# Two score tiles in a row at the start of batch 1, and one pair of transposes moved by a group of tiles

## The chip, the cores and the metric

The kernel runs on one core of one Trainium2 chip. The metric is the device time of a run in microseconds (us). The core has five engines that run side by side, each through its own instructions in order: PE (TensorE, matmuls; its weight loads are shown as PEld), ACT (ScalarE), DVE (VectorE), POOL (GpSimd) and SP (SyncE, which here only issues DMAs).

## What is computed

Attention over 8 batches of 12 heads, 448 rows, 64 columns, with normalised queries and keys, and then two matmuls with a tanh GELU between them:

```python
q_n = q / sqrt(mean(q*q, axis=-1) + 1e-6) * g_q      # k_n likewise with g_k
scores = q_n @ k_n.T / 8                             # per batch and head: 448 x 448
attn = exp(scores - max) / sum                       # softmax over the keys
x = attn @ v                                         # then laid out as 3584 x 768
out = gelu_tanh(x @ w_in) @ w_out                    # 768 -> 2048 -> 768
```

## The kernel before

**Stages.** Batch 0's attention and the first matmul of its rows are written out in a string `FRONT` (L891). From batch 1 on, each batch has two strings of tokens in `STEPS` (L643), split at a bar. The part ahead of the bar is the batch's attention; among its tokens stand pieces of the *second* matmul of the batch before. The part behind the bar is the batch's *first* matmul, and the loop from L957 runs them in turn. The order of these tokens is the program order of every engine: the schedule is manual, so nothing is reordered later, and an engine whose next instruction waits holds up all that stand behind it.

**Tokens** (`run`, L657). `s` makes the next score tile: four matmuls of 64x64 (L335), and one exponential on ACT over 128 x 896 (L326). A batch has 21 tiles, three *chunks* of four heads with seven tiles each, so tile 7 is the first of chunk 1. Below they are s0 to s20, and e0 to e20 are their exponentials. `A1` pops one step of part A of the second matmul of the batch before (four matmuls of 64x64 on 384 columns, L447); `A9` pops nine. `a` adds an exponential into its chunk's running sum on DVE (L362); for the first tile of a chunk it does nothing. `S`, `x`, `R`, `X` are the sums, the products with v, the reciprocals and the scaled results. Every third `s` closes a group of tiles: ahead of its first tile `side` work is issued, behind its last tile `end` work.

**PSUM.** Score tiles, transposes, the second matmul's parts B and on, and the first matmul's tiles share three places of two banks (L305 to L320), handed out strictly in turn. `place` takes the next one; the tile in it waits until the former tile there has been read. Part A lives in two other banks.

**Part A.** Its 32 steps come in two turns of 16. Between them the kernel puts a no-operation on POOL (`turned`, L455 to L457) that waits for PE's 16th step and that the 17th step waits for.

**Heads and chunks.** Pairs of heads are numbered 0 to 5. Pairs 2 and 3 make chunk 1 of keys and queries. In batch 1 their normalised rows are transposed on PE (`both_transposed`, L908: four matmuls of L259 and three or four of L266 into one place), and DVE copies them out (`place_q` L276, `place_k` L285). Chunk 2 of batch 1 is normalised on DVE (`normed`, L247, four instructions), transposed by two DMAs that SP issues (`transposed`, L294 and L290), and SP then issues the four loads of batch 2's first chunk (`loads(2, 0)`, L121 and L138). Its squares are taken on ACT later in the same attention (`squared`, L207).

**What the end of a group does in batch 1's attention** is in the dictionary `here` (L961): entry (g, 0) runs first at the end of group g, (g, 1) last. In the kernel before, both pairs of transposes are run at the end of group 0, behind s2.

Of the kernel before, what the change touches and what calls it, by code (L numbers as in the profile page):

```python
# [16 lines left out]
def kernel(  # L17
# [11 lines left out]
    nc = tc.nc  # L29
# [81 lines left out]
    def slots(j):  # L111
        return slice(0, NK) if j == 0 else slice(NK, NS)
# [71 lines left out]
    def view(n, t, j=None):  # L184

        if n == "q":
            return t if j is None else t[:, 2 * j:2 * j + 2]
        return t if j is None else t[:, :, slots(j)]
# [22 lines left out]
    def stat(t, b, c, n, j=None):  # L211

        if b == 0:
            ns = NQ if n == "q" else NK + j
            at = 14 * j + (0 if n == "q" else 8)
            return t[:P if n == "q" else 128, c, at:at + 2 * ns].rearrange("p (a t) -> p a t", a=2)
        if n == "q":
            s = t[:P, c, :CH * NQ].rearrange("p (h t) -> p h t", h=CH)
            return s if j is None else s[:, 2 * j:2 * j + 2]
        s = t[:, c, CH * NQ:].rearrange("p (a s) -> p a s", a=2)  # L220
        return s if j is None else s[:, :, slots(j)]
# [18 lines left out]
    def normed(b, c, n, j, eng):  # L240
        if (n, b, c) not in nrms:
            shape = [P, 2, NQ, 2, D] if n == "q" else [128, NS, 2, D]
            nrms[n, b, c] = nrmp.tile(shape, BF16, tag=f"nrm{n}", name=f"nrm{n}")
        t = nrms[n, b, c]
        dst = t[:, j] if n == "q" else t[:, slots(j)]
        r = stat(rinvs[b], b, c, n, j)
        eng.tensor_mul(  # L247
            dst.rearrange("p t a d -> p a t d"), view(n, raws[n, b, c], j),
            r.to_broadcast(list(r.shape) + [D]),
        )  # L250

    def trans(b, hp, n, pool, tag=None):
        c, j = hp // 2, hp % 2
        tp = pool.tile([128, 1024], BF16, tag=tag, name="tp") if tag else pool
        if n == "q":
            if hp == 0:
                qT[b] = qkp.tile([128, HP, S], BF16, tag="qT", name="qT")
            for t in range(NQ):
                nc.tensor.transpose(  # L259
                    tp[:, t * P:(t + 1) * P],  # L260
                    nrms[n, b, c][:, j, t].rearrange("p a d -> p (a d)"), ident[:P, :P],
                )
        else:
            s = slots(j)
            for i in range(s.stop - s.start):
                nc.tensor.transpose(  # L266
                    tp[:, i * 128:(i + 1) * 128],
                    nrms[n, b, c][:, s.start + i].rearrange("p a d -> p (a d)"), ident,
                )
        return tp  # L270
# [34 lines left out]
    def place(name):  # L305
        i = unused.pop(0)
        t = spots[i].tile([128, 2, 512], F32, tag="sc", name=name)
        taken.append((t, i))
        return t
# [304 lines left out]
    def m2_parts(b):  # L614
# [26 lines left out]
    homes = []  # L641

    STEPS = {  # L643
# [264 lines left out]
    def both_transposed(b, hp):  # L908

        home = place("tp")  # L910
        tp = home[:, 0].bitcast(BF16)
        for n, at in (("q", 0), ("k", 512)):
            tps[n, b, hp] = trans(b, hp, n, tp[:, at:at + 512])
        place_q(b, hp, tps["q", b, hp], nc.vector)
        place_k(b, hp, tps["k", b, hp], nc.vector)
        leave(home)
# [40 lines left out]
    for b in range(B):  # L957
        m1, side, early, late, here = [], [], [], [], {}
        if b == 0:

            here = {(0, 0): [lambda: both_transposed(1, 2), lambda: rsqrt(1, slice(2, NCH))],  # L961
                    (0, 1): [lambda: both_transposed(1, 3)] +
                            [lambda j=j, n=n: normed(1, 2, n, j, nc.vector)
                             for j in range(2) for n in "qk"] +
                            [lambda: transposed(1, 2)] +
                            [lambda: loads(2, 0)]}
# [114 lines left out]
```

## Time and profile before

| | |
|---|---|
| median of 3 runs | 402.72 us |
| fastest, slowest run | 401.46 us, 403.55 us |
| the profiled execution's own time | 400.14 us |
| its span, first to last instruction | 398.1 us |
| mean granted TensorE clock | 0.994 |
| PE, ACT, DVE, POOL busy | 388.9, 304.1, 243.7, 137.8 us |

In the timeline each row is a start, a duration, an engine, a line, what is written and read, and a count of instructions merged; a bracket gives the engine's idle time before the row and what ended it. Rows of one engine may overlap by some tenths of a microsecond, because its instructions are pipelined: a matmul of 448 columns has a duration of 0.35 us, and the next group can start 0.19 us after it. So PE's stalls are read from the starts of its rows rather than from its busy share.

### The profile page before, as it was taken

What the parts mean: (1) busy time and instruction counts of PE and PEld (TensorE: products, weight loads), DVE (VectorE), ACT (ScalarE), POOL (GpSimd) and SP (SyncE); (2) the same over time, 40 slices, a digit from 0 to 9 for tenths busy, and PEclk for the clock granted to TensorE, in tenths of its full rate; (3) what the DMA queues carried; (4) which work ended last, traced back from release to release, by engine and by line L of the source; (5) the groups of instructions that cost most, each with busy time, mean ns of one, the idle gap of its engine ahead of it and who ended that gap; (6) DMA issues with size and microseconds to landing.
All of it is one profiled execution on the core that took longest, in us unless ns stands there. A gap on an engine that the chain in (4) does not pass through costs nothing.

```text
span 398.1 us, 16991 instructions
## 1 busy us (share of the span) xinstructions
PE 388.9 (98%) x7572; PEld 285.5 (72%) x7572; DVE 243.7 (61%) x409; ACT 304.1 (76%) x409; POOL 137.8 (35%) x166
## 2 busy tenths in 40 slices
PE   7899999999999999999999999999999999999996
PEld 3444557878887678766788888776788889776664
DVE  5889829994897456864489635882399503690010
ACT  4897889968999779976997559985999258984400
POOL 5789002151321772155501646246420740000000
PEclk9899999999999999999999999999999999999999
DMA  8999999997947892939683398749743291210022
GB/s 181 227 237 204 205 204 213 242 252 133 166 105 151 204 192 33 216 84 214 85 160 104 91 215 104 162 130 200 105 66 90 76 122 28 68 56 3 2 81 79
DMA packets 75800, 54.63 MB, mean 137 GB/s; under 512 B 41680, under 2 KB 72272, under 8 KB 75728
## 3 DMA queue, kind: packets, MB, share of 16 engines
q1 hardware_dynamic: 59968, 41.69, 49.7%
q0 software_dynamic: 15440, 11.80, 20.3%
q8 instruction: 59, 0.97, 1.1%
q14 instruction: 13, 0.11, 0.1%
q10 hardware_dynamic: 320, 0.07, 0.1%
HBM read 45.61 MB, written 11.01 MB: 142 GB/s over the span
## 4 chain that ended last, share of the span: by engine, by line
PE 94%; ACT 2%; DMA 1%; SPq 1%; DVE 1%; issue 0%; ACTq 0%; DVEq 0%; POOLq 0%
PE hh L447 27%; PE om L447 17%; PE o L447 13%; PE mm L447 10%; PE sc L335 7%; PE o L552 5%; PE hh L523 4%; PE so L447 4%; ACT ex L326 1%; PE sc L351 1%; PE ox L386 1%; DMA rawk<-in_k_dram 1%; PE o L386 1%; PE h L523 1%; PE tp L266 1%; PE tp L259 1%
## 5 line engine op out<-in xcount | busy, mean ns | idle before, releaser
L326 ACT ACTIVATE ex<-sc,shift 128x896 bf16<-128x896 f32 x168 | 156.8, 1015 | 3.7 <-PE sc L351 2.1
L447 PE MATMUL hh<-xT,win 64*64 64x448 bf16 x2304 | 129.8, 349 | 0.7 <-issue 0.7
L447 PEld LDWEIGHTS <-g 64*64 64x64 bf16 x3072 | 108.4, 107 | 21.4 <-POOLq L456 1.2
L447 PEld LDWEIGHTS <-win 64*64 64x64 bf16 x2688 | 94.5, 106 | 33.7 <-ACTq L456 10.9
L447 PE MATMUL om<-wout,g 64*64 64x384 bf16 x1664 | 103.5, 322 | 0.0
L447 PE MATMUL mm<-wout,g 64*64 64x384 bf16 x704 | 86.0, 323 | 0.1
L447 PE MATMUL o<-wout,g 64*64 64x384 bf16 x704 | 85.2, 323 | 0.3 <-ACT g L532 0.3
L532 ACT ACTIVATE g<-hh 128x896 bf16<-128x896 f32 x55 | 49.7, 915 | 34.2 <-PE hh L447 31.7
L224 DVE TENSOR_REDUCE ss<-sq 128x14 f32<-128x896 f32 (+4 forms) x45 | 48.0, 1081 | 27.5 <-ACT sq L207 27.4
L362 DVE TENSOR_TENSOR es<-es,ex 128x896 bf16<-128x896 bf16 x92 | 57.0, 620 | 9.9 <-ACT ex L326 4.1
L335 PE MATMUL sc<-qT,kT 64*64 64x448 bf16 x600 | 57.0, 352 | 0.1
L920 POOL COPY mark<-es 1x1 bf16<-1x1 bf16 x27 | 8.9, 329 | 129.9 <-DVE es L362 109.4
L247 POOL TENSOR_TENSOR nrmq<-rawq,rinv 112x512 bf16<-112x512 f32 x35 | 36.4, 1054 | 30.7 <-DMA qT<-nrmq 23.7
L247 POOL TENSOR_TENSOR nrmk<-rawk,rinv 128x512 bf16<-128x512 f32 (+1 forms) x34 | 32.1, 959 | 2.3 <-ACT rinv L233 1.3
L362 DVE TENSOR_TENSOR es<-ex 128x896 bf16<-128x896 bf16 x21 | 12.9, 612 | 30.6 <-ACT ex L326 30.3
L447 PE MATMUL o<-xT,win 64*64 64x448 bf16 x192 | 31.5, 349 | 0.0
L447 PE MATMUL mm<-xT,win 64*64 64x448 bf16 x192 | 31.3, 349 | 0.0
L335 PEld LDWEIGHTS <-kT 64*64 64x64 bf16 x600 | 24.5, 106 | 8.3 <-issue 2.4
L300 DVE TENSOR_SCALAR kT<-kT,gcol 128x896 bf16<-128x896 bf16 x19 | 14.8, 777 | 23.7 <-DMA kT<-nrmk 23.7
L447 PEld LDWEIGHTS <-vt 64*64 64x64 bf16 x588 | 20.5, 107 | 6.2
L447 PE MATMUL o<-ex,vt 64*64 64x448 bf16 x182 | 20.8, 349 | 0.0
L447 PE MATMUL mm<-ex,vt 64*64 64x448 bf16 x182 | 20.5, 349 | 0.0
(112 smaller groups left out, 451.3 us busy)
## 6 DMA issues: line engine op xcount, KB each, us to landing
rawq<-in_q_dram SPq DMA_DIRECT2D x48, 224.0 KB, 5.2
rawk<-in_k_dram SPq DMA_DIRECT2D x42, 224.0 KB, 5.3
vt<-in_v_dram POOLq DMA_DIRECT2D x24, 168.0 KB, 4.3
win<-in_moe_w_in_dram POOLq DMA_DIRECT2D x4, 768.0 KB, 12.0
wout<-in_moe_w_out_dram POOLq DMA_DIRECT2D x4, 768.0 KB, 20.9
out_dram<-osb SPq DMA_DIRECT2D x7, 336.0 KB, 4.4
out_dram<-osb SPq DMA_DIRECT2D x8, 288.0 KB, 2.7
out_dram<-osb SPq DMA_DIRECT2D x8, 240.0 KB, 2.6
```

The source lines that it names most:

```text
L224: nc.vector.reduce_sum(stat(ssq[b % 3], b, c, n, j), view(n, sqs[n, b, c], j), axis=AX.X)
L247: eng.tensor_mul(dst.rearrange("p t a d -> p a t d"), view(n, raws[n, b, c], j), r.to_broadcast(list(r.shape) + [D]),)
L300: nc.vector.tensor_scalar(kT[:, c], kT[:, c], gcol[:, 0:1], None, op0=ALU.mult)
L326: latest[:] = [nc.scalar.activation(dst, sc[:, :, :S], AF.Exp, scale=scale, bias=shift)]
L335: nc.tensor.matmul(sc[own(j), a, :S], kT[own(a), c, t, own(j)], qT[b][own(a), 2 * c + j], start=True, stop=True,)
L362: nc.vector.tensor_add(es, exs[b, c, 0] if t == 1 else es, exs[b, c, t])
L386: nc.tensor.matmul(o[a * D:(a + 1) * D], w(a), e[:, a], start=(i == 0), stop=(i + 1 == len(steps)),)
L447: self.last = nc.tensor.matmul(self.outs[k][own(m)], w, e, start=not self.begun[k], stop=self.left[k] == 0,)
L523: nc.tensor.matmul(h[i * m:(i + 1) * m, j, :S], win[:, c // 2 + NCH * (c % 2), f * 128 + i * m:f * 128 + (i + 1) * m], xT[b][:, c], start= ...
L532: nc.scalar.activation(g[:, fs[0]:fs[0] + len(fs), (b % 2) * S:(b % 2 + 1) * S], hs1[fs[0]][:, :, :S], AF.Gelu_apprx_tanh)
L552: nc.tensor.matmul(o[j * m:(j + 1) * m, :HD], g[:, f, i * 128 + j * m:i * 128 + (j + 1) * m], wout[:, f, half * HD:(half + 1) * HD], start ...
L920: nc.gpsimd.tensor_copy(mark, x)
```

## The change

Two things change, both in batch 1's attention.

1. In the string of tokens the beginning is different; all behind it is the same. The number of steps of part A ahead of s5 is 18 in both.

```
before: s A1 a A3 s A6 a A1 s A1 s A2 s A4 s s A2 a s A4 a ...
after:  s s A1 a A9 a s A2 s A2 s A4 s s A2 a s A4 a ...
```

So s1 follows s0 at once, ten steps of A (eleven before) stand ahead of s2, and two steps (one before) stand between s2 and s3.

2. The transposes of pair 3 are run at the end of group 1 (behind s5), no longer at the end of group 0 (behind s2).

```diff
             here = {(0, 0): [lambda: both_transposed(1, 2), lambda: rsqrt(1, slice(2, NCH))],
-                    (0, 1): [lambda: both_transposed(1, 3)] +
-                            [lambda j=j, n=n: normed(1, 2, n, j, nc.vector)
+                    (1, 0): [lambda: both_transposed(1, 3)],
+                    (0, 1): [lambda j=j, n=n: normed(1, 2, n, j, nc.vector)
                              for j in range(2) for n in "qk"] +
                             [lambda: transposed(1, 2)] +
                             [lambda: loads(2, 0)]}
```

The order of the work behind s2 is then, before: transposes of pair 2, of pair 3, four normalisations, two DMA transposes, four loads, s3, s4, s5. After: transposes of pair 2, four normalisations, two DMA transposes, four loads, s3, s4, s5, transposes of pair 3, s6. In the three places the tiles then stand as follows (the places are called a, b, c; "om" is the first tile of part B):

| | s0 | s1 | s2 | pair 2 | pair 3 | s3 | s4 | s5 | s6 | s7 | om | s8 |
|---|---|---|---|---|---|---|---|---|---|---|---|---|
| before | a | b | c | a | b | c | a | b | c | a | b | c |
| after | a | b | c | a | b (behind s5) | b | c | a | c | a | b | c |

2 rows, old and new, of the table STEPS are left out of this document.

## Prediction, made before the changed kernel was run

> **What bounds the kernel now.** First the page, for the whole span: its length, the engines' busy time, and the chain that ended last.
>
> ```profile
> span 398.1 us, 16991 instructions
> PE 388.9 (98%) x7572; PEld 285.5 (72%) x7572; DVE 243.7 (61%) x409; ACT 304.1 (76%) x409; POOL 137.8 (35%) x166
> ...
> PE 94%; ACT 2%; DMA 1%; SPq 1%; DVE 1%; issue 0%; ACTq 0%; DVEq 0%; POOLq 0%
> ```
>
> PE sets the time, so the question is what the change does to PE's stalls, and whether later stalls swallow it. Next the timeline of PE where batch 1's attention begins.
>
> ```profile
> 53.70 0.38 PE L335 MATMUL sc<-qT,kT 64*64 64x448 bf16 x4
> 54.40 0.35 PE L447 MATMUL o<-wout,g 64*64 64x384 bf16 x2 [0.32 <-ACT g L532]
> ...
> 56.72 0.36 PE L259 MATMUL tp<-ident,nrmq 112*128 112x112 bf16 x4
> ...
> 57.62 0.36 PE L259 MATMUL tp<-ident,nrmq 112*128 112x112 bf16 x4 [0.37 <-ACT ex L326]
> ...
> 58.13 0.35 PE L447 MATMUL o<-wout,g 64*64 64x384 bf16 x2
> ...
> 58.52 0.38 PE L335 MATMUL sc<-qT,kT 64*64 64x448 bf16 x4
> ...
> 59.03 0.39 PE L335 MATMUL sc<-qT,kT 64*64 64x448 bf16 x4
> ...
> 60.21 0.55 PE L335 MATMUL sc<-qT,kT 64*64 64x448 bf16 x8
> ```
>
> These rows are s0 at 53.70, part A beginning at 54.40, the transposes of pair 2 at 56.72 and of pair 3 at 57.62, one step of A at 58.13, s3 at 58.52, s4 at 59.03, s5 and s6 at 60.21. PE stalls several times here: its starts are further apart than its work is long. Now ACT in the same stretch.
>
> ```profile
> 51.59 0.92 ACT L532 ACTIVATE g<-hh 128x896 bf16<-128x896 f32 x1 [0.41 <-PE hh L523]
> ...
> 55.66 2.80 ACT L326 ACTIVATE ex<-sc,shift 128x896 bf16<-128x896 f32 x3
> ...
> 58.71 0.23 ACT L233 ACTIVATE rinv<-lg 128x30 f32<-128x30 f32 x1
> 58.95 6.40 ACT L326 ACTIVATE ex<-sc,shift 128x896 bf16<-128x896 f32 x7
> ...
> 65.55 1.07 ACT L326 ACTIVATE ex<-sc,shift 128x896 bf16<-128x896 f32 x1
> 67.10 0.55 ACT L406 ACTIVATE rb<-so 128x448 f32<-128x448 f32 x1 [0.47 <-DVE st L393]
> ...
> 72.57 0.63 ACT L207 ACTIVATE sq<-rawq 112x512 f32<-112x512 f32 x1 [0.20 <-DMA rawq<-in_q_dram]
> ```
>
> The rows are the last GELU of a two-bank tile, e0 to e2, the second of two small instructions that give chunk 2's reciprocal roots, e3 to e9, e10 (behind a copy), the first reciprocal by logarithm, and the second square of batch 2. From 55.66 to 66.62 ACT is in work but for tenths. **ACT bounds this opening**, and its start hangs on batch 0's last GELU and the change of tables behind it, which are not touched. Three exponentials take 2.80 us and seven 6.40, so they follow each other every (6.40 - 2.80)/4 = 0.90 us and one lasts 2.80 - 1.80 = 1.00. The ends of e0, e1, e2 are thus 56.66, 57.56, 58.46, and of e3 to e7 59.95, 60.85, 61.75, 62.65, 63.55. PE follows such an end by about 0.05 (57.62 behind 57.56, 58.52 behind 58.46).
>
> **The change, part by part.** It adds and removes no instruction; eight PE transposes, two DVE copies, one score tile and three steps of A change places. Prices on PE come from the chain of waits.
>
> ```profile
> 70.40 0.19 PE sc L335 x4
> 70.58 1.62 PE om L447 x40
> ```
>
> A score tile holds PE for 0.19 us, a step of A or B for 1.62/10 = 0.162 us. Pair 3's transposes hold it from 57.62 to the next row at 58.13, 0.51 us; pair 2's, with one matmul less, an estimated 0.44.
>
> *s1 behind s0.* PE was idle from 53.89 (53.70 + 0.19) to 54.40, where A waits for the last GELU. s1 now fills 0.19 us of it at no cost. That s1's place is free I take from the GELUs of two-bank tiles: the last began at 51.59 and was over by 52.51. The gain is lost at once, because ten steps of A and s2 end at 54.40 + 1.62 + 0.19 = 56.21, and pair 2 still waits for e0 until 56.72.
>
> *s3 and s4.* Pair 2 ends at 57.16, two steps of A at 57.49; s3 waits for e1: 57.62 (before 58.52). Two steps more, then s4 waits for e2: 58.52 (before 59.03). ACT cannot use either: e3 begins behind the reciprocal roots at 58.95 in any case.
>
> *The gate on POOL.* Step 16 ends earlier by 0.51 us with s4, so the gate passes and s5 begins 0.51 earlier: 59.70. What POOL has queued behind the gate (a one-element copy and a load of v) only comes earlier.
>
> *DVE.*
>
> ```profile
> 58.14 0.38 DVE L276 COPY qT<-tp 128x448 bf16<-128x448 bf16 x1
> ...
> 58.77 0.38 DVE L276 COPY qT<-tp 128x448 bf16<-128x448 bf16 x1
> 59.07 0.47 DVE L285 TENSOR_SCALAR kT<-tp,gcol 128x512 bf16<-128x512 bf16 x1
> 59.46 0.68 DVE L247 TENSOR_TENSOR nrmq<-rawq,rinv 112x512 bf16<-112x512 f32 x1
> ...
> 61.73 2.07 DVE L362 TENSOR_TENSOR es<-es,ex 128x896 bf16<-128x896 bf16 x3
> ...
> 66.42 0.64 DVE L393 STREAM_TRANSPOSE st<-so 128x448 f32<-128x448 f32 x1
> ```
>
> Pair 2's copies (from 58.14) stay. Then stood pair 3's, at 58.77 and 59.07, which hid the wait for the reciprocal roots (58.94). Now the normalisations come next and begin at 58.98: the same DVE work is 58.98 - 58.77 = 0.21 us late. The four take 61.73 - 59.46 = 2.27, so pair 3's copies begin at 61.25 and end at 61.63 (q) and 62.02 (k), the first sum of exponentials at 61.94. All later DVE work is 0.21 late.
>
> *Pair 3 and its consumers, the new wait.* Pair 3 has place b behind s3, so it waits for e3 (59.95): 60.00 to 60.51, a stall of about 0.1. s6 is in c behind s4: it waits for e4, 60.90 to 61.09, a stall of 0.39. Two steps of A, 61.42. s7 is the first tile of chunk 1: it reads pair 3's queries, which DVE has at 61.63, and its place waits for e5 (61.75): s7 at 61.80, a stall of 0.38. Behind s7 stand seven steps of A and two of B: 61.80 + 0.19 + 9 x 0.162 = 63.45, so **s8 begins at 63.45, where before it began at 62.70: 0.75 late.**
>
> *ACT.* e7 is not hurt (s7 ends at 62.18, e6 runs until 62.65). e8 now waits for s8: 63.45 + 0.38 + 0.05 = 63.88; by the spacing of the row it was 58.95 + 5 x 0.90 = 63.45. It is 0.43 late, and so are e9, the copy and e10, which then ends at 67.05. The reciprocal by ACT at 67.10 had been idle for 0.47 us until DVE's transposition was over (66.42 + 0.64); that comes 0.21 later, so L406 begins at 67.31, and ACT is only **0.21 late**. The square at 72.57 had waited 0.20 for its load: the load is issued 0.48 sooner (next part), so ACT is level again at 73.1.
>
> *SP.* The DMA transposes follow the normalisations.
>
> ```profile
> 61.35 1.34 SPq L294 DMA_TRANSPOSE qT<-nrmq  x1
> ```
>
> The normalisations come 59.46 - 58.98 = 0.48 sooner, and with them two DMA transposes and four loads. All are moved past pair 3, which issues no DMA; nothing else in SP's queue is passed. I cost this at nothing: the first to wait is the square above, for 0.20. Bounds: 0.25 gained if that wait is all that held PE at 74.14, 0.2 lost if the load lands as before (72.57) and nothing is swallowed.
>
> *What swallows the 0.75.* From s8 on, PE stalls where it waited for exponentials or sums.
>
> ```profile
> 62.70 0.38 PE L335 MATMUL sc<-qT,kT 64*64 64x448 bf16 x4
> ...
> 64.79 0.85 PE L447 MATMUL om<-wout,g 64*64 64x384 bf16 x16
> ...
> 65.56 0.38 PE L447 MATMUL so<-es,ones 64*64 64x448 bf16 x4
> ...
> 68.45 0.82 PE L447 MATMUL om<-wout,g 64*64 64x384 bf16 x16
> ...
> 69.20 0.38 PE L335 MATMUL sc<-qT,kT 64*64 64x448 bf16 x4
> ...
> 73.20 0.85 PE L447 MATMUL om<-wout,g 64*64 64x384 bf16 x16
> ...
> 74.14 0.38 PE L335 MATMUL sc<-qT,kT 64*64 64x448 bf16 x4
> ```
>
> The first row is s8. In each pair behind it PE was ready a step's 0.162 per four matmuls after the first row, at 65.44, 69.10 and 73.85. The stalls are 0.12, 0.10 and 0.29, together 0.51: PE is 0.75 - 0.51 = **0.24 late at s16**, if ACT is level there. Behind it ACT has nothing late and PE one stall more:
>
> ```profile
> 85.42 0.32 PEld L447 LDWEIGHTS <-win 64*64 64x64 bf16 x9 [1.08 <-issue]
> ```
>
> and the page's group of these matmuls:
>
> ```profile
> L447 PE MATMUL hh<-xT,win 64*64 64x448 bf16 x2304 | 129.8, 349 | 0.7 <-issue 0.7
> ```
>
> The group's idle time in the whole span is this one stall; from there on PE has work until the end, and what is late stays late. Nothing the profile names ended it. If it belongs to a place in the program, 0.24 passes through; if to a moment, 0.24 vanishes. I take the first, being the nearer to a stall without a releaser, and round: **+0.2 us**.
>
> One rule of the Trainium skill bears on that stall: Runtime: NRT & Kernel Launch, section "Instruction fetch mechanics", says that an engine's instructions are fetched in blocks of 16 KiB through a DMA queue of its own, mostly hidden. The page's instruction queue agrees in size (a row of packets, MB and share: 59 packets of together 0.97 MB, 16 KB each); by that rule a stall is either none or tied to the program, and the sum would stay +0.2.
>
> ```profile
> q8 instruction: 59, 0.97, 1.1%
> ```
>
> **Sum.** 400.14 + 0.2 = 400.3 for the profiled execution. That execution lies 2.6 us below the median of the runs, so I carry the difference over: 402.7 + 0.2 = 402.9.
>
> **The rivals.**
>
> 1. *The slip is carried whole.* If pair 3's copies or s7 come later than I have them, ACT loses its slack at 67.10 and 72.57 and PE keeps the 0.75: 403.5. For it speaks that three stalls take the place of two; against, the three stalls and two gaps of ACT named above. Chance 0.17.
> 2. *The sooner loads win.* ACT's 0.20 at 72.57 goes, e15 comes sooner, and PE's 0.29 at 74.14 with it: -0.3, 402.4. Against: DVE and PE are late there. 0.13.
> 3. *The stall at 85.42 changes* by its own length, up to 1.08 either way, if it hangs on the loads' traffic: 401.8 or 404.0. 0.10.
> 4. *Slower by the clock.* PE now stalls in five or six short pieces from 56.2 to 61.8. In this trace a stretch with PE little busy was followed by one at half clock:
>
> ```profile
> 7.50:11.00 3.50, 1.60 (x15) 1.03 (x14) 2.59 (x9) 1.86 (x6) 2.58 (x4) 1.00 1.19 218
> 11.00:14.50 3.50, 3.50 (x21) 1.76 (x21) 2.48 (x6) 2.62 (x4) 3.28 (x4) 0.51 1.37 222
> ...
> 57.10:60.50 3.40, 2.88 (x55) 1.73 (x56) 2.90 (x7) 3.35 (x6) 0.56 (x1) 1.00 1.32 204
> ```
>
> (columns: stretch, length, busy time and count of PE, PEld, DVE, ACT, POOL, then granted clock.) Once at 0.51 for 3.5 us costs 3.5 x 0.49 = 1.7, with the 0.2 above 1.9; a second one 3.6. It decides if PE's busy share there falls to that of the first row, 46%; it is 85% before, and I expect some 75%. 0.04, at 404.8.
> 5. *The change doesn't do what it says*: s1 finds its place taken and waits. Then A is late too, by at most s1's 0.19, ahead of a wait for e0: 402.9 still. 0.02.
>
> **How the numbers follow.** My forecast, -0.1 to +0.5 around 402.9, has 0.54. The median of three runs moves by itself (401.46 to 403.55 before); 0.5% is 2.0 us, about what a measurement of this kernel can tell from no change. No single case but the clock's second window passes 2.0; case 3, the clock, and the runs' own spread together give slower 0.10 and faster 0.07. The range goes from the fastest run before, 401.46, rounded to 401.4, to the slowest with the whole slip, 403.55 + 0.75 = 404.3.
>
> **What would show it right or wrong.** Right: s3 at 57.6; pair 3 between s5 and s6 near 60.0; s7 near 61.8; s8 near 63.45; an ACT gap of 0.4 ahead of e8; the first rb of ACT near 67.3; the DMA transposes near 60.9; s16 0.2 late. Wrong: s7 held by DVE's copies past 62.0; e0 later than 55.7; the end of PE's stall at 85.42 moved by over 0.3; any stretch under full clock between 55 and 85.

## The result, and the profile after

| | before | after |
|---|---|---|
| median of 7 runs each | 402.72 us | 405.42 us |
| fastest, slowest run | 401.44, 403.55 us | 404.23, 407.60 us |
| ratio, with its 95% interval | | 1.0081 [1.0052, 1.0111] |
| the profiled execution's span | 398.1 us | 403.4 us |

The changed kernel is slower, by 2.1 to 4.5 us of some 402. The two profiled executions differ by more, 5.3 us, because that of before was a quick one (400.14 us, under all seven in the table; that of after, 405.42, is its median). First the page of after: span, busy time, and the chain that ended last.

```profile
span 403.4 us, 16991 instructions
PE 388.3 (96%) x7572; PEld 284.3 (70%) x7572; DVE 245.0 (61%) x409; ACT 304.7 (76%) x409; POOL 137.3 (34%) x166
...
PE 81%; DMA 13%; POOL 2%; issue 2%; SPq 1%; DVE 0%; ACTq 0%; ACT 0%; DVEq 0%; POOLq 0%
```

As many instructions, and PE is busy as long as before (388.3 and 388.9 us): the span grew by idle time of PE. The 13% of "DMA" in the chain says nothing of this growth: the chain goes back through one short wait for the last weights of the second matmul, at 65.88, to their transfer (26.55 us from 39.29) and to the loads at the program's start. "Issue", which is time with no releaser, grew from 0% to 2%. Next PE's waits from 54 to 95 us, from where batch 1's attention begins (columns: us in total, times, longest).

```profile
PE om L447 <- issue: 4.0, 2, 2.5
PE sc L335 <- issue: 1.4, 1, 1.4
PE sc L335 <- ACT ex L326: 0.6, 3, 0.2
PE tp L259 <- ACT ex L326: 0.3, 1, 0.3
```

The last two rows are the forecast waits for exponentials. The first two were forecast by no step: three stalls, together 5.4 us, that nothing in the profile ended ("issue"). Where they are, the timeline of PE says:

```profile
69.50 0.35 PE L335 MATMUL sc<-qT,kT 64*64 64x448 bf16 x1 [1.35 <-issue]
...
77.53 0.51 PE L447 MATMUL om<-wout,g 64*64 64x384 bf16 x5 [2.45 <-issue]
...
84.83 0.67 PE L447 MATMUL om<-wout,g 64*64 64x384 bf16 x9 [1.58 <-issue]
```

Each is *inside* something that has no wait inside it: the first ahead of a score tile's last matmul (x1; the other three had run), the other two inside a step of four. From start to start they last 1.70, 2.77 and 1.90 us, together 6.37. Before had one such stall, at 85.42, which takes 1.00 from start to start. The rest of PE's time is untouched; here are the stretches around the stalls, first of before and then of after (columns: stretch, length, PE busy and count, granted clock, DMA share, which is a sum over packets and can pass 1, GB/s).

```profile
62.00:70.00 8.00, 8.00 (x184) 1.00 1.25 216
70.00:78.00 8.00, 7.91 (x189) 1.00 1.11 246
78.00:86.00 8.00, 7.35 (x162) 1.00 1.12 280
86.00:94.00 8.00, 8.00 (x173) 1.00 0.85 193
```

```profile
62.00:70.00 8.00, 6.51 (x147) 1.00 1.26 159
70.00:78.00 8.00, 5.55 (x136) 1.00 1.11 247
78.00:86.00 8.00, 6.42 (x152) 1.00 1.17 248
86.00:94.00 8.00, 8.00 (x177) 1.00 0.59 153
```

Each of the first three stretches has lost PE work, at full clock. Of the 5.3 us, 6.37 - 1.00 = 5.37 are these stalls; the whole execution also began 0.29 sooner (e0 at 55.37, before 55.66), which leaves 5.3 - 5.37 + 0.29 = 0.2 for everything else.

**What a stall without a releaser is here.** Count the records of PE and PEld, the few of their sequencer included, in order of time and from 0. In after the three stalls are ahead of records 1217, 1473 and 1729, the one of before ahead of 1985. All are 256n + 193, so neighbours are 256 apart. The page has a queue whose packets have just that size (columns: packets, MB, share):

```profile
q8 instruction: 59, 0.97, 1.0%
```

59 packets are 0.97 MB, so 16384 bytes each. 59 x 256 = 15104, and PE and PEld together have 15166 records; in a run below with 208 records more there are 60 packets. So the packets are PE's own code, 256 instructions in each. In executions without stalls such a packet begins when PE is near record 256(n + 1), and PE needs it some 200 records (about 4.6 us) later. The packets of four *blocks* against the moment at which PE was ten records ahead of 256(n + 1) ("passed", worked out from the records; the request itself isn't recorded), below called the block's moment. The stalls are from start to start, and a packet's end is given where the text uses it:

```
             before                              after
block   passed  packet         stall      passed  packet         stall
3       62.71   63.32 - 64.29  0          63.03   66.88 - 68.07  1.70
4       68.45   from 69.18     0          70.61   74.72 - 76.04  2.77
5       74.15   from 75.58     0          78.56   81.99 - 83.35  1.90
6       79.56   82.25 - 83.64  1.00       85.89   from 87.41     0.03
```

Before, a block begins 0.6, 0.7, 1.4 and 2.7 us after that moment; only the last is too late. After, three begin 3.85, 4.1 and 3.4 us after it, and each of the four stalls, before's too, ends 1.4 to 1.8 us behind its packet's end. What came ahead of block 3 is in the timeline of SP's queue, first of before, then of after (the row is the DMA's issue).

```profile
61.35 1.34 SPq L294 DMA_TRANSPOSE qT<-nrmq  x1
62.79 1.98 SPq L290 DMA_TRANSPOSE kT<-nrmk  x1
```

```profile
60.58 1.34 SPq L294 DMA_TRANSPOSE qT<-nrmq  x1
62.02 1.38 SPq L290 DMA_TRANSPOSE kT<-nrmk  x1
63.50 0.58 SPq L121 DMA_DIRECT2D rawq<-in_q_dram  x1
```

Before, the block's moment (62.71) lies ahead of the second transpose (62.79). After, PE reaches it later (63.03) and the DMAs come sooner: both transposes are already out. The first of them leaves 62.71 - 61.35 = 1.36 us ahead of the moment before, and 63.03 - 60.58 = 2.45 us after.

### The profile page after: what moved, and what is told of

Its sections match the earlier page's. It is cut to its first block, busy times and chain, and to the rows that moved or that the text cites. A ratio compares the mean times of both kernels' runs of the same rounds, so it can differ in the third digit from the quotient of the medians.

```text
span 403.4 us, 16991 instructions
## 1 busy us (share of the span) xinstructions
PE 388.3 (96%) x7572; PEld 284.3 (70%) x7572; DVE 245.0 (61%) x409; ACT 304.7 (76%) x409; POOL 137.3 (34%) x166
## 4 chain that ended last, share of the span: by engine, by line
PE 81%; DMA 13%; POOL 2%; issue 2%; SPq 1%; DVE 0%; ACTq 0%; ACT 0%; DVEq 0%; POOLq 0%
PE hh L447 27%; PE om L447 17%; PE o L447 12%; PE mm L447 10%; PE sc L335 7%; DMA wout<-in_moe_w_out_dram 7%; DMA rawk<-in_k_dram 6%; PE o L552 5%; PE so L447 4%; POOL wout L766 1%; SPq L121 1%; PE o L588 0%; POOL sq L209 0%; POOL win L760 0%; SPq L154 0%
## 5 line engine op out<-in xcount | busy, mean ns | idle before, releaser
L447 PE MATMUL om<-wout,g 64*64 64x384 bf16 x1664 | 105.0, 323 | 4.2 <-issue 4.0
L335 PE MATMUL sc<-qT,kT 64*64 64x448 bf16 x600 | 58.5, 352 | 1.9 <-issue 1.4
```

Source lines behind the costliest of these rows:

```text
L335: nc.tensor.matmul(sc[own(j), a, :S], kT[own(a), c, t, own(j)], qT[b][own(a), 2 * c + j], start=True, stop=True,)
L447: self.last = nc.tensor.matmul(self.outs[k][own(m)], w, e, start=not self.begun[k], stop=self.left[k] == 0,)
```

## The experiments

The theory: blocks of PE's instructions are fetched behind DMAs that are in flight, and the change put three of them behind more DMAs. The main rival: the new order of tiles, through places, exponentials or DVE, costs the time, and the stalls are how it is shown. Within the theory it is open which DMAs matter: transposes or loads. All ratios are to the kernel before in the same session, with 95% intervals. Stalls are counted from start to start.

**The two parts apart.** x1_order has only the new tokens, x2_pair only the later transposes of pair 3 (in both the other part is as before):

```diff
 x1_order, against after
...
-                    (1, 0): [lambda: both_transposed(1, 3)],
-                    (0, 1): [lambda j=j, n=n: normed(1, 2, n, j, nc.vector)
+                    (0, 1): [lambda: both_transposed(1, 3)] +
+                            [lambda j=j, n=n: normed(1, 2, n, j, nc.vector)
...
 x2_pair, against after
-        s s A1 a A9 a s A2 s A2 s A4 s s A2 a s A4 a ...
+        s A1 a A3 s A6 a A1 s A1 s A2 s A4 s s A2 a s A4 a ...
```

> The new order of tokens alone; pair 3 is transposed behind s2 as before. Three theories of the 5.3 us that the profiled span grew by. BLOCKS: PE's instructions come in blocks of 256 (16 KB) through a DMA queue, and PE stands still, without a semaphore to wait for, at its 1217th, 1473rd, 1729th and 1985th row when a block is late (1.70, 2.78 and 1.91 us at the first three in the changed kernel, 1.00 us at the fourth alone in the kernel before); a block is late when the DMA transposes and loads are ahead of it. ORDER: the waits between the engines that the prediction counted are simply larger. CHANCE: the last weights landed 1.15 us later in the profiled run of the changed kernel (65.84 against 64.69), by the start of that run. Here DVE's work stands as before, so the DMA transposes leave at 61.0 to 61.5 as before: BLOCKS expects no stall at row 1217 and a time of 0.997 to 1.003 of before. ORDER expects at most 0.3 us, as two of the three new waits need the moved pair. CHANCE expects 1.000.

> The pair's move alone; the tokens as before. DVE normalises about 0.5 us sooner, so the DMA transposes leave at about 60.6 to 60.9, while PE reaches the place where it asks for the fourth block (row 1020) no sooner than before (62.7) and likely some tenths later. BLOCKS expects stalls without a releaser at rows 1217 and 1473 of 1 us or more, and 1.005 to 1.011 of before. ORDER expects the prediction's slip of 0.2 to 0.8 us (1.000 to 1.002) and no such stall. CHANCE expects 1.000.

Measured: x1_order 0.9992 [0.9966, 1.0017], x2_pair 1.0071 [1.0043, 1.0099]. PE's waits for nothing, x1_order first:

```profile
PE hh L447 <- issue: 0.8, 1, 0.8
```

```profile
PE om L447 <- issue: 3.8, 2, 1.9
PE sc L335 <- issue: 0.9, 1, 0.9
```

The tokens cost nothing; the move of pair 3 is the whole loss, and its stalls are again ahead of records 1217, 1473 and 1729 (1.28, 2.22, 2.17). In x1_order the second transpose is issued at 63.36 and the block's moment is 63.26, as in before. This ties the loss to one part, and doesn't yet tell the theory from its rival.

**Other borders between the blocks, same order.** The kernel opens with idle matmuls. More of them, made shorter, put the same work at other places in its blocks: 64 records in x3_after_52, 208 in x4_before_124.

```diff
 x3_after_52, against after
-    idle(20, ps_m.tile([128, 512], F32, tag="mm", name="w")[:, :S])
+    idle(52, ps_m.tile([128, 512], F32, tag="mm", name="w")[:, :172])
 x4_before_124, against before
-    idle(20, ps_m.tile([128, 512], F32, tag="mm", name="w")[:, :S])
+    idle(124, ps_m.tile([128, 512], F32, tag="mm", name="w")[:, :72])
```

> The changed kernel with 52 warm-up matmuls of 172 columns on zeros in place of 20 of 448 at the very start: the same columns, 64 more rows on PE, and so every later place at which PE asks for a block comes 64 rows sooner. BLOCKS: the fourth block is asked for at about 61.7 in place of 63.0, before the transposes' packets flow (from 63.4), so the first stall (now at row 1217 again, 64 rows sooner in the program) is gone or under 0.5 us; the next two blocks are asked for at 66 to 67 and 71 to 72, in the midst of the loads, so they may stay late; 0.998 to 1.006 of before, and in any case stalls at other places of the program than in the changed kernel. ORDER and CHANCE: the place of the rows in the program doesn't matter, 1.008 as for the changed kernel.

> The kernel before with 124 warm-up matmuls of 72 columns in place of 20 of 448: 208 more rows on PE, so its blocks are asked for 208 rows sooner, which is 48 rows later than before for the block in question (about 63.8 to 64.0 in place of 62.7). Nothing else of the work differs from before. BLOCKS: that block now stands behind the transposes' packets (from 63.0), PE stalls for 0.5 to 2.5 us about 197 rows after it has asked, and later ones may follow; 1.002 to 1.012 of before. ORDER and CHANCE: 1.000.

Measured: x3_after_52 1.0027 [0.9995, 1.0059], x4_before_124 1.0000 [0.9972, 1.0027]. In x3_after_52 the stall ahead of record 1217 is gone: PE passes block 3's moment at 62.93, and the block begins at 63.85. Later stalls remain (1.15, 1.62, 1.16), in a trace of an execution of 405.17 us. They stand ahead of records 1473, 1729 and 1985, and those of x4_before_124 ahead of 1985 and 2241, so 256n + 193 again although the work at each record is another: the stalls keep to the count of instructions and not to the place in the schedule. That they are late blocks of code rests on this and on the packets. The median of x3_after_52, 402.24, has most of the loss back although the order is that of after, which speaks against the rival; its interval still touches that of after. x4_before_124 missed: the block that was put behind the DMAs began only 1.1 us late, with no stall; the stalls came two and three blocks later (1.19 and 0.79). So a block among these DMAs isn't late by rule.

**The order of after, the DMAs later.** y1_hold issues the two transposes and the loads behind them at the end of group 1, the first held on e5 (the lines by which `transposed` holds it aren't shown); y3_loads leaves the transposes and holds the loads until e8.

```diff
 y1_hold, against after
...
-                            [lambda: transposed(1, 2)] +
-                            [lambda: loads(2, 0)]}
+                            []}
+            here[1, 1] = [lambda: transposed(1, 2, True), lambda: loads(2, 0)]
 y3_loads, against after
-                            [lambda: transposed(1, 2)] +
-                            [lambda: loads(2, 0)]}
-            late = [(2, lambda: loads(2, 1, True)), (3, lambda: gain(1, 2)), (4, lambda: loads(2, 2, True))]
+                            [lambda: transposed(1, 2)]}
+            late = [(2, lambda: loads(2, 0, True)), (2, lambda: loads(2, 1, True)), (3, lambda: gain(1, 2)), (4, lambda: loads(2, 2, True))]
```

> The changed kernel, with the two DMA transposes and the four loads of batch 2 behind them issued at the end of group 1 and the first transpose held until s5's exponential is done (about 0.8 us later than the normalisation that it waited for). PE's rows are as in the changed kernel. So far: the order of tokens alone cost nothing, the pair's move alone 0.7%, and each stall of 0.8 us or more without a releaser, in six traces, ended at a PE row of 256 n + 193. What makes the block late? TRANSPOSES: their packets. In the changed kernel the first transpose leaves 2.45 us ahead of row 1014, before it 1.36 us. With 0.8 us taken off that (1.6 to 1.7 us), the fourth block should start before or soon behind their first packets and the stall at row 1217 be under 0.5 us; 1.000 to 1.004 of before. LOADS: they leave later by the same 0.8 us, so it expects the same here. WEIGHTS (the last of w_out, still landing at 65 to 66 us, holds the block up): no change, 1.4 us or so at row 1217 and 1.007.

> The changed kernel, with the four loads of batch 2's first chunk held until e8 is done (to leave at about 64.5 in place of 63.5); the transposes leave as in the changed kernel (60.6 and 62.0). The fourth block is asked for at about 63.0, so no load is issued then. TRANSPOSES and WEIGHTS: the block still starts 3 us or more after row 1014 and PE stalls for 1 us or more at row 1217; 1.005 to 1.010 of before. LOADS: the block starts within about 1 us and the stall at row 1217 is gone, 1.000 to 1.004.

Measured: y1_hold 1.0020 [0.9985, 1.0055], y3_loads 1.0111 [1.0072, 1.0150]. PE's waits of y1_hold (its lines are one number lower), and its transposes:

```profile
PE sc L334 <- ACT ex L325: 1.1, 4, 0.5
PE hh L446 <- issue: 0.9, 1, 0.9
```

```profile
61.70 1.33 SPq L293 DMA_TRANSPOSE qT<-nrmq  x1
63.14 1.24 SPq L290 DMA_TRANSPOSE kT<-nrmk  x1
```

With the same order of tiles and the DMAs 1.1 us later, the three stalls are gone; one of before's kind is left (1.22 ahead of record 1985). The last weights land at 65.82, as in after (65.84), so it isn't they that hold block 3 up. PE even waits longer for exponentials, and that costs nothing that can be measured. y3_loads is mixed: its stall ahead of 1217 is 0.25, where the theory that transposes alone hold a block up wanted at least 1. Whether the loads are part of it isn't shown by this: the block begins 2.2 us after its moment, and so it does in u_spread, below, where these loads leave as in after. In the next places y3_loads has 1.59 and 2.73.

**Two plain copies in place of the transposes** (y4_copies), and **after once more** (z_after2, one execution):

```diff
 y4_copies, against after
+    def copied(b, c):
+        src = nrms["k", b, c].rearrange("p s a d -> p (s a d)")
+        nc.sync.dma_start(qT[b][:, 2 * c:2 * c + 2].rearrange("p h s -> p (h s)"), src)
+        nc.sync.dma_start(kT[:, c].rearrange("p t s -> p (t s)"), src)
...
-                            [lambda: transposed(1, 2)] +
+                            [lambda: copied(1, 2)] +
```

> The changed kernel, with the two DMA transposes of batch 1's chunk 2 replaced by two plain copies of the normalised keys into the same tiles, so chunk 2 of batch 1 is computed from other numbers (that part of the computation is changed). Two DMAs of the same size in bytes leave at about the same moments, but not as transposes. TRANSPOSES: the fourth block starts within 1.5 us of row 1014, no stall of over 0.5 us at row 1217, and less at the next ones; 0.997 to 1.004 of before. LOADS and WEIGHTS: the stall at row 1217 stays at 1 us or more, 1.005 to 1.010.

> The changed kernel once more, for a second trace. BLOCKS: stalls without a releaser again at rows 1217, 1473 and 1729, together 4.5 to 6.5 us, whatever the moment at which the last weights land. CHANCE: other stalls, as the start of the run goes.

Measured: y4_copies 1.0015 [0.9968, 1.0062]. Its ten executions spread from 399.21 to 406.81 us, with a median of 404.83 that lies higher than the ratio says, and its trace, of 405.39 us, has stalls of 0.29, 3.29 and 0.25; so it settles nothing about what a transpose adds over a copy. z_after2 took 405.13 us, with 0.92, 2.23 and 2.72 ahead of the same three records, so they aren't the chance of one execution. In it PE passed block 3's moment at 63.66 and the block began at 63.93, but its packet lasted 3.57 us instead of about 1: it was held up in mid-transfer.

**What the traces have in common.** Over the first ten traces I counted, from block 2 on, the DMAs issued and not yet landed when PE was 24 records ahead of 256(n + 1), and took each block's delay from there. With none in flight (139 blocks) no block began over 0.45 us later. With nine or more (13 blocks) they began 2.6 to 4.9 us later, and 12 of the 13 were followed by a stall of 1 us or more. The count says less than it seems: of blocks 0 and 1, eleven have nine or more in flight too, and none began over 1.3 us later; and block 3 of after, the first of the loss, had only four in flight (three in before) and began 4.1 us later. In the six traces taken after the count, four more blocks had nine or more in flight: they began 1.3 to 4.1 us later, and one stalled for over 1 us. Four experiments follow from the count.

**In before, the loads ahead of the transposes** (v_early) should make the stalls of after; **in before, batch 3's loads later** (w_late30) should take away the one at 85.42; **in after, the other loads of batch 2 further apart** (u_spread) should take away the later stalls. z_before2 is one more execution of before.

```diff
 v_early, against before
-                            [lambda: transposed(1, 2)] +
-                            [lambda: loads(2, 0)]}
+                            [lambda: loads(2, 0, True)] +
+                            [lambda: transposed(1, 2)]}
 w_late30, against before
-            m1 += [(-1, lambda: gpsimd_waits(newest[0][:1, 0, :1])),
+            m1 += [(-1, lambda: loads(3, 0, True)),
+                   (-1, lambda: gpsimd_waits(newest[0][:1, 0, :1])),
...
-            side.append(((6, 5, 3)[min(b, 2)], lambda: loads(b + 3, 0, True)))
+            if b:
+                side.append(((6, 5, 3)[min(b, 2)], lambda: loads(b + 3, 0, True)))
 u_spread, against after
-            late = [(2, lambda: loads(2, 1, True)), (3, lambda: gain(1, 2)), (4, lambda: loads(2, 2, True))]
+            late = [(4, lambda: loads(2, 1, True)), (3, lambda: gain(1, 2)), (6, lambda: loads(2, 2, True))]
```

> The kernel before, its PE rows unchanged, with the four loads of batch 2's first chunk ahead of the two DMA transposes on SP and held until e2 is done, so that they leave at about 58.6 to 61 in place of 64.9 to 66.8. A count over the ten traces so far: where no DMA was in flight when PE came near a block's end (24 rows ahead of a multiple of 256) the block started at once (never over 0.5 us late); with eight it was 2.3 us late on average, with nine or more 2.6 to 4.9 us, and 12 of those 13 were followed by a stall of 1 us or more. BLOCKS: with the loads sooner the fourth block finds 7 or more in flight in place of 3, so it is 1.5 us late or more and stalls or near stalls follow at rows 1217 and 1473; stalls without a releaser between rows 1000 and 2000 add up to 2 us or more (1.0 in the kernel before), 1.002 to 1.010 of before. ORDER: PE's order and its waits for ACT and DVE are those of before, 1.000.

> The kernel before, with the four loads of batch 3's first chunk issued behind batch 1's attention (with the first of the after-attention work) and not ahead of its last group. In the traces of before, of the new order alone and of the held transposes the one stall left is 1.0 to 1.2 us at row 1985, whose block is asked for with nine or ten DMAs in flight, four of them these loads. BLOCKS: five or six are in flight there, the stall at row 1985 goes, and no other comes; 0.995 to 0.999 of before, faster than both kernels. If the loads only crowd the next block, a stall at row 2241 takes its place and it is 1.000.

> The changed kernel, with the loads of batch 2's second chunk two groups later (held until e14) and those of its third chunk two groups later too; the transposes and first loads as in the changed kernel. BLOCKS: the stall at row 1217 stays (0.9 to 1.7 us: that block waits with two transposes in flight), those at rows 1473 and 1729 (2.2 to 2.8 and 1.9 to 2.7) shrink to under 1 us each, as four or five DMAs are in flight there in place of nine; 1.001 to 1.006 of before. If the stalls at 1473 and 1729 only follow from the first stall, whatever is in flight, they stay, 1.008.

> The kernel before once more, for a second trace. BLOCKS: one stall without a releaser in batch 1's attention or just behind it, at row 1985, about 1 us; none of 1 us at rows 1217, 1473 or 1729.

Measured: v_early 1.0126 [1.0096, 1.0156], w_late30 0.9982 [0.9957, 1.0008], u_spread 1.0062 [1.0033, 1.0092], z_before2 401.67 us. PE's longest wait of v_early, then two waits of u_spread, then the two of z_before2:

```profile
PE om L447 <- DMA wout<-in_moe_w_out_dram: 4.2, 1, 4.2
```

```profile
PE hh L447 <- issue: 1.9, 1, 1.9
PE om L447 <- DMA wout<-in_moe_w_out_dram: 1.4, 1, 1.4
```

```profile
PE hh L447 <- issue: 1.1, 1, 1.1
PE om L447 <- issue: 0.4, 1, 0.4
```

v_early missed its mechanism: it is slower, but through a wait that has a name. The loads held back the last weights of the second matmul (landed at 69.40), and PE, standing still for 4.49 us from start to start, gave the blocks time to come; none holds PE up. w_late30 did what was expected of the stall (none in its trace up to 1985, span 397.7), but the gain isn't clear of no change. u_spread, in a trace of an execution of 407.33 us (its median is 403.70), has no stall ahead of 1217, but not because its block came in time (it began 2.2 us after its moment): PE had stood still for 1.74 us ahead of it for the last weights (landed at 67.55). The next two stalls shrank to 0.84 and 0.53, and one of 2.27 came ahead of 1985. Whether the moved loads did this isn't shown by one such trace. z_before2 shows that the stalls of before vary: 0.72 ahead of record 1729 and 1.44 ahead of 1985, together 2.16.

**Both cures in the changed kernel.** t_both is after with the edits of y1_hold and w_late30; z_after3 is after again, beside it.

> The changed kernel with both shifts of DMAs at once: batch 1's transposes and the loads behind them held until e5 is done (as in the run with the held transposes), and batch 3's first loads behind batch 1's attention (as in the run with the late loads). PE's order is that of the changed kernel. BLOCKS: no stall of 1 us or more at rows 1217, 1473, 1729 or 1985; the time is that of the late loads on the kernel before, 0.995 to 1.001 of before, so the new order by itself is within 0.2% of the old one. ORDER: the new waits on ACT and DVE remain and cost what the changed kernel cost, 1.005 or more.

> The changed kernel beside it, on the same chip: stalls without a releaser at rows 1217, 1473 and 1729 of 4 to 6.5 us together, 1.005 to 1.011 of before.

Measured: t_both 1.0005 [0.9976, 1.0035], z_after3 1.0081 [1.0048, 1.0115]. PE's waits from 54 to 95 us, t_both first:

```profile
PE sc L334 <- ACT ex L325: 0.6, 3, 0.2
PE tp L259 <- ACT ex L325: 0.3, 1, 0.3
```

```profile
PE om L447 <- issue: 3.2, 2, 1.9
PE sc L335 <- issue: 0.7, 1, 0.7
PE sc L335 <- ACT ex L326: 0.6, 3, 0.2
PE tp L259 <- ACT ex L326: 0.3, 1, 0.3
```

The waits for exponentials, which are the cost of the new order, are the same in both to a tenth; the stalls without a releaser (1.08, 1.68 and 2.18 ahead of the three records in z_after3) are there or not there, and the time goes with them. The intervals don't overlap. The trace of t_both is of an execution of 399.56 us, under its median of 401.41; whether the others have stalls no trace shows. t_both is no faster than before either, so the new order gains nothing once it is freed of the stalls. Since it also holds back batch 3's loads, it is to be set beside w_late30 too: 1.0005 against 0.9982, so the new order may cost some 0.2% of its own, which these intervals can't tell from nothing.

## Why the prediction was wrong

*The order of the engines: right.* With the 0.29 by which the execution began sooner taken off, the forecasts are met. PE, in the timeline of after:

```profile
57.33 0.38 PE L335 MATMUL sc<-qT,kT 64*64 64x448 bf16 x4
...
58.23 0.38 PE L335 MATMUL sc<-qT,kT 64*64 64x448 bf16 x4 [0.19 <-ACT ex L326]
...
59.69 0.37 PE L259 MATMUL tp<-ident,nrmq 112*128 112x112 bf16 x4
...
60.49 0.38 PE L335 MATMUL sc<-qT,kT 64*64 64x448 bf16 x4 [0.20 <-ACT ex L326]
...
61.39 0.39 PE L335 MATMUL sc<-qT,kT 64*64 64x448 bf16 x4 [0.19 <-ACT ex L326]
...
63.03 0.39 PE L335 MATMUL sc<-qT,kT 64*64 64x448 bf16 x4
```

s3, s4, pair 3, s6, s7 and s8 were forecast, less 0.29, at 57.33, 58.23, 59.71, 60.61, 61.51 and 63.16. From s6 on they came 0.12 sooner than that. s8 is 63.03 - (62.70 - 0.29) = 0.62 late, forecast 0.75. On ACT, e3 was forecast at 58.95 - 0.29 = 58.66, the gap ahead of e8 at 0.43, and the first reciprocal at 67.31 - 0.29 = 67.02:

```profile
58.55 4.58 ACT L326 ACTIVATE ex<-sc,shift 128x896 bf16<-128x896 f32 x5
63.47 1.91 ACT L326 ACTIVATE ex<-sc,shift 128x896 bf16<-128x896 f32 x2 [0.34 <-PE sc L335]
...
67.30 0.54 ACT L406 ACTIVATE rb<-so 128x448 f32<-128x448 f32 x1 [0.65 <-DVE st L393]
```

They came at 58.55 (which gives 0.11 of s6's 0.12), 0.34 and 67.30. Ahead of the reciprocal, which is 0.28 late, PE had a wait that the prediction doesn't have:

```profile
65.06 1.33 PE L447 MATMUL om<-wout,g 64*64 64x384 bf16 x16
```

Sixteen such matmuls took 0.85 in before (64.79). Here they stood 0.46 at 65.88, until just behind the landing of the second matmul's last weights (65.84). The change isn't shown to make this wait: z_before2 has 0.46 at the same place.

*The DMAs: the step that failed.* Their moment was right to the hundredth: forecast 0.48 sooner, 61.35 - 0.48 - 0.29 = 60.58, measured 60.58. The failed step is its price: "I cost this at nothing: the first to wait is the square", with bounds of 0.25 gained and 0.2 lost. The runs showed 5.37 us of stalls in its place in the profiled execution, and 2.70 us between the medians. The prediction asked only who waits for these transfers to *land*. Nothing in it asked who else has to get *past* them. The transposes came 0.48 sooner, PE passed block 3's moment 0.62 later, and the two add up to the 1.1 us by which the first transpose's lead over the moment grew, from 1.36 to 2.45 us. Block 3 then began 3.85 us after its moment, and PE stalled. The lead tells the traces apart better than the moment's place behind both transposes, which y1_hold and t_both share with after: in six traces with a lead of 2.45 us the packet of block 3 ended 3.1 to 5.0 us after the moment, in seven with 1.15 to 1.7 us it ended 0.8 to 2.6 us after it. Two stand apart: x4_before_124, whose block among these DMAs has 2.44 and 2.0 us, and v_early, where the loads are ahead as well, with 1.43 and 3.1 us. Why the next two blocks were late too, whether through the loads that came behind or through the first stall, isn't shown. That the moved DMAs, and not the moved tiles, make the loss is shown by t_both beside z_after3, and y1_hold agrees.

*The stall at 85.42: misread.* "If it belongs to a place in the program, 0.24 passes through; if to a moment, 0.24 vanishes." It belongs to both: the count of instructions gives the records at which it can fall, and the DMAs at that moment have a say in whether it falls (the traces of w_late30 and t_both, with batch 3's loads later, have none at record 1985; those of before, z_before2, x1_order and y1_hold have 1.00 to 1.44). Each of the two, taken alone, made it a matter of tenths. In after that place stalls for 0.03 and three earlier ones for 6.37. The rule of the Trainium skill that I quoted (Runtime: NRT & Kernel Launch, "Instruction fetch mechanics") fits in the size of a block; its "mostly hidden" holds for 56 of this trace's 59 packets, and the other three are the whole result. My reading of it, that the sum would stay at +0.2, was wrong. That 0.29 + 5.3 - 5.37 = 0.2 is left beside the stalls is no proof of the forecast's +0.2, as the stalls also swallow PE's later waits: that ahead of s16, at 74.14 in before, is gone in after.

*The rivals.* The third named the mechanism ("if it hangs on the loads' traffic") but bound its price by the one stall that before shows, 1.08. The price of one stall here is 0.25 to 3.3 us, and there can be a stall every 256 records. The slip (0.62 of 0.75) and the sooner loads decided nothing. The clock stayed at 1.00 from 54 to 94 us. The time given for one slow window, 404.8, counts the +0.2 twice: 402.72 + 1.9 = 404.6.

*Still open.* Which of the DMAs in flight holds a block up, and for how long in a single case. The count of DMAs in flight separates the extremes, but not block 3 of after (four in flight, 3.85 us after its moment) from the block of x4_before_124 (four, 1.1 us); in t_both a block with nine in flight made no stall; and the run with copies in place of transposes was inconclusive. When PE asks for a block isn't recorded, only when it passes a record.

## What to carry to other kernels

An engine that stands still in the middle of a group, with no releaser, at distances of 256 instructions, was here waiting for its own code: put the instruction queue's packets beside it before it is explained by the schedule. When an edit moves a DMA, or the engine's position against one, by even half a microsecond, ask which instruction block is fetched in that time, and not only who waits for the data. To tell such a loss from one of the order, keep the order and move the DMAs (here 1.0081 became 1.0020 with batch 1's transposes and the loads behind them held, and 1.0005 with batch 3's loads later as well), and time several executions of both kernels, since one stall varies by up to a microsecond.

## What the runs showed of the hardware

The lead of PE's instruction fetch is short in time: where PE ran freely, about 200 records, 4.6 us at some 45 records per us, from the block's moment to the first record that needs it. In this stretch a packet of 16 KB took 0.9 to 1.6 us, once 3.57, and after a stall PE went on 1.2 to 1.8 us behind its end, so a block that begins some 2 us after its moment can already be too late. With no DMA in flight blocks were never over 0.45 us late; with nine or more most were, by 2.6 to 4.9 us in the first ten traces, with the exceptions named above. And 64 more instructions of PE at the very start of the program, 50 us ahead of the stalls, came with a median of 402.24 us for the changed kernel in place of 405.42, each against its own 401.77 and 402.72 for before; the two intervals still touch.
